# Reordering the prologue's loads: channel weights four tiles ahead, inputs before the first weight tile, five table buffers

## The chip, the core and the metric

The kernel runs on one core of a Trainium2 chip. It uses the core's five engines: TensorE (PE) for matrix products, VectorE (DVE) and ScalarE (ACT) for elementwise work and copies, GpSimd (POOL) for some elementwise work and for starting transfers, SyncE (SP) for starting transfers. Each engine works through its own list of instructions in the order in which the program gives them, and waits on semaphores for what the other engines and the transfers deliver. The metric is the device time of one execution in microseconds (us). Before the change it is 2592.13 us, the median of three runs (2591.88 to 2593.12).

## The reference

Two layers follow one another, on a batch of 8 sequences of 3008 positions by 256 features. The first multiplies each sequence's real Fourier spectrum by a filter. The second is a mixer block: a product along the positions, then one along the features.

```python
X = np.fft.rfft(x, axis=1)
y = np.fft.irfft(X * (filt_r + 1j * filt_i)[None], n=3008, axis=1)       # 8 x 3008 x 256

h  = np.maximum(y.transpose(0, 2, 1) @ w_tok1, 0.0) @ w_tok2             # 3008 -> 256 -> 3008
u  = y + h.transpose(0, 2, 1)
out = u + np.maximum(u @ w_ch1, 0.0) @ w_ch2                             # 256 -> 1536 -> 256
```

The weights arrive as 64-bit floats, seen by the kernel as pairs of 32-bit words, and have to be turned into 32-bit floats on the chip.

## The kernel before

The Fourier transforms are done as two small dense transforms (64 and 47 points) by TensorE. The kernel has two parts. A **prologue** transforms the first sequence (`dft(GROUPS[0])`), converts all weights and computes the first token products; then `mix` runs the mixer over all 8 sequences, with the transforms of the following sequences (`dft(GROUPS[1])` and so on) interleaved step by step.

**The weight tiles.** The weights are cut into 40 tiles, each handled by a Python generator with three stages: *begin* takes a staging buffer and starts the load, *copy* lets ScalarE read the high words, *end* lets VectorE finish the conversion (and, for channel weights, start what follows). Every call of `convert()` ends one tile, copies the next, and begins another.

```python
early = [(up, "u")] * 2 + [(tp, "t")] * 2 + [(vp, "v")] * 2
late = [(t2p, "t2"), (t3p, "t3")]                       # each pool has 2 buffers: 4 in all
stages = [(t4p, "t4")] * (A // 2) + early * 3 + late * 5     # 12 + 18 + 10 tiles

tiles = ([w1_load(i) for i in range(A // 2)] + [w2_load(i) for i in range(TC * N2 // NG)]   # 12 + 16
         + [wc1_load(c * (DC // 512), False) for c in range(DH)] + [f(i) for f, i in LAST]) # 2 + 10
begin, copy, end = iter(tiles), iter(tiles), iter(tiles)

def convert():
    ended[0] += 1
    while behind and behind[0][0] < ended[0] - 2:       # products of earlier tiles on TensorE
        behind.pop(0)[1]()
    advance(end)
    advance(copy)
    advance(begin)
```

Counting all calls of `advance(begin)`, six more than the number of converted tiles have been begun at any time: `convert()` number n ends tile n-1 and begins tile n+5 (tiles counted from 0). Tiles 30 to 39 (`LAST`) are staged in the four `t2` and `t3` buffers in turn, so tile 34 takes the buffer of tile 30.

**The channel weights.** Tiles 28 to 39 hold `w_ch1` and `w_ch2`. The mixer uses a fast matrix scheme with seven products, which needs sums of weight blocks. GpSimd makes them (`combine`, five operations for each of the 6 block columns `jp`, once for `chan[0]` and once for `chan[1]`). GpSimd also starts these tiles' loads.

```python
def combine(w):                                          # lines 331 to 339
    a11, a12, s4, na22, s3, s2, s1 = (w[:, :, n, :] for n in range(7))
    add = nc.gpsimd.tensor_tensor
    nc.gpsimd.tensor_scalar(out=na22, in0=s1, scalar1=-1.0, scalar2=None, op0=ALU.mult)   # L335
    add(out=s1, in0=s3, in1=s1, op=ALU.add)              # L336
    add(out=s3, in0=a11, in1=s3, op=ALU.subtract)        # L337
    add(out=s2, in0=s1, in1=a11, op=ALU.subtract)        # L338
    add(out=s4, in0=a12, in1=s2, op=ALU.subtract)        # L339

def wc1_load(i, late=True):
    c, q = divmod(i, DC // 512)
    st = stage(512)
    for g in range(CB):                                  # four loads, on GpSimd's queue (L345)
        nc.gpsimd.dma_start(st[ts(g, CW)], moe_w_ch1[ds((g * DH + c) * CW, CW), ts(q, 512)])
    yield
    yield from rounded(st, 512, [...], late)             # DVE L247 to L252, sum in L273
    if c == DH - 1:
        for jp in range(2 * q, 2 * q + 2):
            combine(chan[0][:, jp:jp + 1])

def wc2_load(i):                                         # one load (L356), one combine of chan[1]
    ...
```

**The first transform.** Twelve input tiles are loaded, half of each tile by SP and half by GpSimd; TensorE multiplies each (L419), ScalarE copies the result into `turned` (L422), and after six and after twelve tiles VectorE transposes half of `turned` (L459, eight instructions). Then 32 steps follow: `b_unit(k)` (L475 on TensorE, the products with the filter L487 to L489 on VectorE) and `bi_unit(k)` (L499 on TensorE, copy L505 on ScalarE). Each pair of steps needs a filter tile (`filt_load`, on GpSimd's queue, 3 buffers) and a table tile (`wb`, on SP's queue, 3 buffers).

```python
        def w_load(c):
            ...
                wbs[g] = wbp.tile([P, WC, P + KR], FP32, tag="wb", name="wb")
                nc.sync.dma_start(wbs[g], (wbi0_d if first else wbi_d)[:, ts(g, WC), :])
            filt_load(c, first)
        ...
        for k in range(K2 + 1):
            if k < K2:
                b_unit(k)
                if k % KC == 0 and k // KC + 2 < K2 // KC:
                    t2_load(k // KC + 2)
                    w_load(k // KC + 2)
                if first and k % KC == KC - 1 and k + 1 < K2:
                    filt_double(k // KC + 1)             # ACT L225
            if k >= 1:
                bi_unit(k - 1)
            yield
```

**The prologue's order.**

```python
        advance(begin)                                    # tile 0, ahead of the inputs
        for i, _ in enumerate(dft(GROUPS[0])):            # tile 1 is begun after six input tiles
            ...
            if i < NXC:                                   # NXC = 12 input tiles
                if i in (0, 2, 4, 6):
                    advance(begin)
                if i == 0:
                    advance(copy)
                if i in (NXC // 2 - 1, NXC - 1):
                    convert(); rounds += 1
            else:
                if (i - NXC) % 3 == 2:                    # eleven times in the 32 steps
                    convert(); rounds += 1
                k = i - NXC - 2
                if 19 <= k < 25:
                    t4_load(0, k - 19, 0, PARTS[1])       # into the buffers that staged tiles 5 to 10
                ...
        sum_up()
        for i in range(rounds, A // 2 + TC * N2 // NG):   # the rest, up to 28 converted tiles
            convert()
            ...
            if i == A // 2 + BY_PE - 1:
                sum_up()
                acc = token_sums(0)
        h1s[0] = token_relu(acc)
        for dh in range(DH):
            convert()                                     # tiles 28 and 29
            u_part(0, 0, dh)
```

In `mix`, each of the 6 x 6 items of a sequence is one `up_first` (L602), `up_middle`, `up_last` (L618), and the `down` products of the item before (L636); `convert()` is called twice in each item, ahead of `up_first` and ahead of `up_last`, until tile 39 is done (five items). VectorE's elementwise instructions of the mixer all stand in line 580.

Of the kernel before, what the change touches and what calls it, by code (L numbers as in the profile page):

```python
# [10 lines left out]
FP32 = mybir.dt.float32  # L11
# [12 lines left out]
P = 128  # L24
K2 = 32
A = 24
KR = 4 * A
HALF = 64
XC = 2
NXC = A // XC  # L30
# [3 lines left out]
KC = 2  # L34
WC = 2
# [89 lines left out]
def kernel(  # L125
# [32 lines left out]
    t1p = pool("t1p", 2)  # L158
    wbp = pool("wbp", 3)
# [48 lines left out]
    def filt_load(c, first):  # L208
        t, k0 = filts[c % FB], c * KC

        q = nc.gpsimd if first else nc.sync
        for src, i, p0 in ((filt_r, 0, 0), (filt_i, 1, HALF)) + (() if first else ((filt_r, 0, HALF),)):
            q.dma_start(t[p0:p0 + A, i], raw(src, k0, [[64 * D, A], [D, KC], [1, D]]))
            lo = p0 + 32
            if k0 == 0:
                q.dma_start(t[lo:lo + A, i, 0, :], raw(src, 32, [[64 * D, A], [1, D]]))
            k = max(k0, 1)

            for j0, n in ((0, 16), (16, A - 1 - 16)):
                q.dma_start(t[lo + j0:lo + j0 + n, i, k - k0:KC, :],  # L220
                            raw(src, 64 * (j0 + 1) - k, [[64 * D, n], [-D, k0 + KC - k], [1, D]]))
# [54 lines left out]
    ended = [0]  # L276
# [98 lines left out]
    def advance(it):  # L375
        s = next(it, None)
        if s:
            next(s, None)
# [5 lines left out]
    def convert():  # L384

        ended[0] += 1
        while behind and behind[0][0] < ended[0] - 2:
            behind.pop(0)[1]()
        advance(end)
        advance(copy)  # L390
        advance(begin)

# [22 lines left out]
    def a_unit(b, c):  # L417
        ps = bank(free_bank())
        nc.tensor.matmul(ps, wa0 if b == 0 else wa, xs.pop((b, c)).rearrange("p a d -> p (a d)"), start=True, stop=True)  # L419
        if b == 0:  # L420
            d0, c = divmod(c, NXC // 2)
            nc.scalar.copy(out=turned[:, ts(c, 2 * XC), ds(d0 * P, P)], in_=ps.rearrange("p (a d) -> p a d", d=P))  # L422
            return
        t1 = t1p.tile([P, XC, D], FP32, tag="t1", name="t1")
        nc.scalar.copy(out=t1.rearrange("p a d -> p (a d)"), in_=ps)
        nc.scalar.dma_start(rows_of(z_d, b)[:, ts(c, XC), :], t1)

    def dft(bs):
        first = bs[0] == 0
        nb = len(bs)  # L430
        todo = [(b, c) for b in bs for c in range(NXC)]
        wbs = {}

        def w_load(c):
            if c * KC % WC == 0:
                g = c * KC // WC
                wbs[g] = wbp.tile([P, WC, P + KR], FP32, tag="wb", name="wb")
                nc.sync.dma_start(wbs[g], (wbi0_d if first else wbi_d)[:, ts(g, WC), :])
            filt_load(c, first)

        ahead = NXC if first else XB
        for u in todo[0:ahead]:
            x_load(*u)
            if first and u[1] == NXC // 2 - 1:
                advance(begin)
        if not first:
            yield True
        for i, u in enumerate(todo):
            if first and i in (1, 4):
                w_load(i // 4)  # L450
            a_unit(*u)
            if i + ahead < len(todo):
                x_load(*todo[i + ahead])
            yield i + 1 < len(todo)
            if first and (i + 1) % (NXC // 2) == 0:

                for d in range(i // (NXC // 2) * P, (i + 1) // (NXC // 2) * P, 16):
                    v = turned.rearrange("p s d -> p d s")[:, d:d + 16, :]
                    nc.vector.transpose(v, v)  # L459
        t2s, t3s, prods = {}, {}, {}  # L460

        def t2_load(c):
            if first:
                return
            t2s[c] = t2p.tile([KR, KC, nb, D], FP32, tag="t2", name="t2")
            for i, b in enumerate(bs):
                nc.sync.dma_start(t2s[c][:, :, i, :], z_d[b, ts(c, KC)].rearrange("k r d -> r k d"))

        def b_unit(k):
            tag = ("b", "pg")[k % 2] if first else free_bank()  # L470
            if not first:
                held.append(tag)
            ps = bank(tag).rearrange("p (b d) -> p b d", b=2)[:, 0:nb, :]
            t2 = turned[:, k, :].unsqueeze(1) if first else t2s[k // KC][:, k % KC]
            nc.tensor.matmul(ps, wbs[k // WC][0:P if first else KR, k % WC, 0:P], t2, start=True, stop=True)  # L475
            re, im = slice(0, HALF), slice(HALF, P)
            t = filts[k // KC % FB]
            fr = t[:, 0, k % KC, :].unsqueeze(1).to_broadcast([P, nb, D])
            fi = t[im, 1, k % KC, :].unsqueeze(1).to_broadcast([HALF, nb, D])
            p1 = p1p.tile([P, 2 if first else nb, D], FP32, tag="p1", name="p1")  # L480
            if first:
                p1, p2 = p1[:, 0:1], p1[:, 1:2]
                prods[k] = (p1, p2)
            else:
                p2 = p2p.tile([P, nb, D], FP32, tag="p2", name="p2")
                prods[k] = (p1,)
            nc.vector.tensor_tensor(out=p1, in0=ps, in1=fr, op=ALU.mult)  # L487
            nc.vector.scalar_tensor_tensor(out=p2[re], in0=ps[im], scalar=-1.0, in1=fi, op0=ALU.mult, op1=ALU.mult)
            nc.vector.tensor_tensor(out=p2[im], in0=ps[re], in1=fi, op=ALU.mult)  # L489
            if not first:  # L490
                nc.vector.tensor_tensor(out=p1, in0=p1, in1=p2, op=ALU.add)  # L491

        def bi_unit(k):


            ps = bank("acc" if first else held.pop(0)).rearrange("p (b d) -> p b d", b=2)[:, 0:nb, :]
            parts = prods.pop(k)
            for i, p in enumerate(parts):
                nc.tensor.matmul(ps[0:KR], wbs[k // WC][:, k % WC, P:], p, start=(i == 0), stop=(i == len(parts) - 1))  # L499
            c, r = divmod(k, KC)  # L500
            if r == 0:
                where, tag = (p2p, "p2") if first and c % 3 == 2 else (t3p, "t3")
                t3s[c] = where.tile([KR, KC, nb, D], FP32, tag=tag, name="t3")

            nc.scalar.copy(out=t3s[c][:, r].rearrange("p b (e g i) -> p b g e i", e=DH, i=CW),  # L505
                           in_=ps[0:KR].rearrange("p b (g e i) -> p b g e i", e=DH, i=CW))
            if r == KC - 1:
                t3 = t3s.pop(c)
                for i, b in enumerate(bs):
                    nc.scalar.dma_start(g_d[b, ts(c, KC)].rearrange("k r d -> r k d"), t3[:, :, i, :])  # L510

        for c in range(2):
            t2_load(c)
            if not first:
                w_load(c)
        yield
        yield
        if first:
            filt_double(0)
        for k in range(K2 + 1):  # L520
            if k < K2:
                b_unit(k)
                if k % KC == 0 and k // KC + 2 < K2 // KC:
                    t2_load(k // KC + 2)
                    w_load(k // KC + 2)
                if first and k % KC == KC - 1 and k + 1 < K2:
                    filt_double(k // KC + 1)
            if k >= 1:
                bi_unit(k - 1)
            yield  # L530
# [241 lines left out]
    with tc.manual_schedule():  # L772
# [3 lines left out]
            nc.vector.memset(t, 0.0)  # L776
        rounds = 0
        second = dft(GROUPS[1])
        advance(begin)
        for i, _ in enumerate(dft(GROUPS[0])):  # L780
            if i == 0:
                for t, src in ((wai_t, wait_d), (wa, wa_d), (wai, wai_d), (ident, ident_d)):
                    nc.scalar.dma_start(t, src)

            if i < NXC:
                if i in (0, 2, 4, 6):
                    advance(begin)
                if i == 0:
                    advance(copy)
                if i in (NXC // 2 - 1, NXC - 1):  # L790
                    convert()
                    rounds += 1
            else:
                if (i - NXC) % 3 == 2:
                    convert()
                    rounds += 1

                k = i - NXC - 2
                if 19 <= k < 25:
                    t4_load(0, k - 19, 0, PARTS[1])  # L800
                elif k == 25:
                    next(second)
                elif k in (30, 31):
                    for c in range(3):
                        t4_load(0, 3 * (k - 30) + c, PARTS[1], PARTS[2])
# [68 lines left out]
```

## Time and profile before

| what | value |
| --- | --- |
| time, median of three | 2592.13 us |
| span of the profiled execution | 2589.4 us |
| TensorE busy, share of the span | 2508.9 us, 97% |
| VectorE busy | 1814.0 us, 70% |
| ScalarE busy | 691.1 us, 27% |
| GpSimd busy | 533.0 us, 21% |
| TensorE in us 0 to 40 | 17.78 us |
| TensorE in us 40 to 114 | 67.92 us of 74 |
| TensorE in us 161 to 229 | 50.88 us of 68, at a mean granted clock of 0.82 |
| TensorE in us 229 to 300 | 69.07 us of 71 |

The page of the profile gives the engines' busy times, the waits and the chain of work that ended last; the trace behind it gives every instruction with its start, its duration, the idle time before it and what ended that idle time. The span falls into a first stage (inputs, us 0 to 37), the 32 steps of the first transform (to about 114), the rest of the weights with the token products (to about 160), and the mixer.

### The profile page before, as it was taken

The page shows a single profiled execution, that of the slowest core. Times are in us where ns is not written, and L with a number is a line of the kernel's source. Part 1 is how long each engine was busy: PE and PEld are TensorE (multiplying, and loading weights), DVE is VectorE, ACT ScalarE, POOL GpSimd, SP SyncE. Part 2 cuts the span into 40 slices and gives each one's busy share as a digit, 9 for nine tenths or more (in the row PEclk, how much of TensorE's full clock was granted, in tenths as well). Part 3 has the DMA queues.
Part 4 walks back from the last instruction along what each step waited for, and adds up shares of the span by engine and source line. Part 5 has one row for each costly group of instructions (what it writes and reads, how often), then busy time and mean ns, then how long its engine had stood idle before and what let it go on. Part 6 is the DMA issues. An engine that isn't in the chain of part 4 may idle for free.

```text
span 2589.4 us, 31456 instructions
## 1 busy us (share of the span) xinstructions
PE 2508.9 (97%) x10952; PEld 2004.6 (77%) x10952; DVE 1814.0 (70%) x3458; ACT 691.1 (27%) x1347; POOL 533.0 (21%) x980
## 2 busy tenths in 40 slices
PE   6979999999999999999999999999999999999998
PEld 3556766788878777888787777788888888888887
DVE  7886888556675888746666788846678577647676
ACT  3423222123222222222221222212222122212222
POOL 5552111111211112112112111121121121211212
PEclk8989999999999999999999999999999999999999
DMA  9854333312332322203232223211232121100000
GB/s 214 234 155 140 110 101 110 106 48 86 94 90 63 88 84 75 80 15 91 90 95 78 75 84 86 81 31 57 90 85 74 50 64 53 25 9 8 17 12 21
DMA packets 153739, 205.21 MB, mean 79 GB/s; under 512 B 34232, under 2 KB 104994, under 8 KB 153580
## 3 DMA queue, kind: packets, MB, share of 16 engines
q1 hardware_dynamic: 82332, 114.08, 15.4%
q0 software_dynamic: 31296, 41.51, 6.6%
q10 hardware_dynamic: 39952, 47.61, 5.7%
q8 instruction: 87, 1.43, 0.2%
q14 instruction: 72, 0.59, 0.1%
HBM read 131.23 MB, written 71.83 MB: 78 GB/s over the span
## 4 chain that ended last, share of the span: by engine, by line
PE 79%; DVE 12%; DMA 3%; issue 2%; ACT 2%; POOL 1%; ACTq 0%; SPq 0%; DVEq 0%; POOLq 0%
PE ps_po L636 27%; PE ps_pg L602 16%; PE ps_pg L618 12%; PE ps_b L562 4%; PE ps_b L545 3%; DVE t L580 2%; PE ps_acc L545 2%; PE ps_acc L562 2%; DVE hh L580 2%; PE ps_acc L499 2%; PE ps_b L567 2%; PE ps_acc L419 2%; DVE u L580 1%; PE ps_b L499 1%; PE ps_b L475 1%
## 5 line engine op out<-in xcount | busy, mean ns | idle before, releaser
L580 DVE TENSOR_TENSOR hh<-ps_pg,s 128x512 f32<-128x512 f32 (+3 forms) x864 | 482.4, 586 | 633.9 <-ACT s L605 629.8
L681 POOL DMA_DIRECT2D out_dram<-r x757 | 411.2, 552 | 1947.1 <-ACT hh L623 928.6
L623 ACT ACTIVATE hh<-hh 128x512 f32<-128x512 f32 (+1 forms) x576 | 347.8, 621 | 1127.3 <-DVE hh L580 1127.3
L636 PE MATMUL ps_po<-t,wc 128*128 128x256 f32 (+1 forms) x2304 | 535.5, 375 | 5.0 <-DVE t L580 4.2
L636 PEld LDWEIGHTS ps_po<-t,wc 128*128 128x128 f32 x2304 | 434.5, 190 | 132.5 <-issue 53.5
L602 PE MATMUL ps_pg<-v,wc 128*128 128x256 f32 (+1 forms) x1728 | 416.2, 377 | 9.1 <-POOL wc L338 9.0
L636 PE MATMUL ps_po<-hh,wc 128*128 128x256 f32 (+1 forms) x1728 | 414.6, 376 | 6.0 <-POOL wc L339 5.7
L602 PEld LDWEIGHTS ps_pg<-v,wc 128*128 128x128 f32 x1728 | 328.4, 191 | 50.3 <-POOL wc L338 9.8
L636 PEld LDWEIGHTS ps_po<-hh,wc 128*128 128x128 f32 x1728 | 328.2, 190 | 45.9 <-POOL wc L339 6.8
L618 PE MATMUL ps_pg<-u,wc 128*128 128x256 f32 (+1 forms) x1152 | 295.1, 379 | 2.7 <-DVE hh L580 2.3
L580 DVE TENSOR_TENSOR t<-t,hh 128x256 f32<-128x256 f32 (+1 forms) x576 | 242.0, 420 | 19.8
L618 PEld LDWEIGHTS ps_pg<-u,wc 128*128 128x128 f32 x1152 | 217.0, 191 | 38.7 <-DVE hh L580 12.0
L580 DVE TENSOR_TENSOR s<-ps_pg,hh 128x512 f32<-128x512 f32 (+1 forms) x288 | 196.0, 681 | 32.3 <-PE ps_pg L602 1.8
L580 DVE TENSOR_TENSOR t<-hh 128x512 f32<-128x512 f32 (+1 forms) x288 | 192.0, 667 | 0.6 <-ACT hh L623 0.6
L602 PE MATMUL ps_pg<-u,wc 128*128 128x256 f32 (+1 forms) x576 | 169.9, 377 | 0.9 <-DVE hh L580 0.9
L618 PE MATMUL ps_pg<-v,wc 128*128 128x256 f32 (+1 forms) x576 | 169.7, 376 | 0.0
L605 ACT COPY s<-ps_pg 128x256 f32<-128x256 f32 (+1 forms) x288 | 106.0, 368 | 160.2 <-PE ps_pg L602 157.0
L618 PEld LDWEIGHTS ps_pg<-v,wc 128*128 128x128 f32 x576 | 109.2, 191 | 13.5
L602 PEld LDWEIGHTS ps_pg<-u,wc 128*128 128x128 f32 x576 | 102.6, 191 | 19.2 <-issue 8.9
L562 PE MATMUL ps_b<-w,h 128*128 128x512 f32 (+1 forms) x232 | 108.8, 592 | 0.0
L545 PE MATMUL ps_b<-t,w 128*128 128x256 f32 x480 | 104.5, 379 | 0.7 <-DMA t<-g_tmp 0.7
L499 PE MATMUL ps_acc<-p,wb 128*96 128x256 f32 (+1 forms) x256 | 95.0, 471 | 8.0 <-DVE p L491 3.7
(104 smaller groups left out, 2252.6 us busy)
## 6 DMA issues: line engine op xcount, KB each, us to landing
g_tmp<-t ACTq DMA_DIRECT2D x128, 192.0 KB
out_dram<-r POOLq DMA_DIRECT2D x698, 32.0 KB, 1.8
x<-in_x_dram SPq DMA_DIRECT2D x173, 128.0 KB
z_tmp<-t ACTq DMA_DIRECT2D x84, 256.0 KB
t<-z_tmp SPq DMA_DIRECT2D x112, 192.0 KB
t<-g_tmp SPq DMA_DIRECT2D x42, 512.0 KB
wb<-wbi_t SPq DMA_DIRECT2D x80, 224.0 KB
filt<-in_filt_r_dram SPq DMA_DIRECT2D x128, 48.0 KB
```

What stands on the lines that cost most here:

```text
L419: nc.tensor.matmul(ps, wa0 if b == 0 else wa, xs.pop((b, c)).rearrange("p a d -> p (a d)"), start=True, stop=True)
L499: nc.tensor.matmul(ps[0:KR], wbs[k // WC][:, k % WC, P:], p, start=(i == 0), stop=(i == len(parts) - 1))
L545: nc.tensor.matmul(acc[:, t, :], w1[:, a, ts(t, P)], t4[b, a // TC4][:, a % TC4, :], start=(a == 0 and t == 0), stop=(a == A - 1 and t == ...
L562: nc.tensor.matmul(ps[:, 0:w], h1[:, t, ts(dh, P)], w2[:, t, ds(m * 512, w)], start=(t == 0), stop=False)
L567: nc.tensor.matmul(ps[:, ds(q * P, n)], t4[b, c][:, r, ts(dh, P)], wai[:, 0:n], start=False, stop=(q == 3))
L580: nc.vector.tensor_tensor(out=out, in0=in0, in1=in1, op=op)
L602: nc.tensor.matmul(ps[:, 0:hw], chan[0][:, jp, n, :], mov, start=True, stop=True)
L605: nc.scalar.copy(out=s[:, 0], in_=g[0][:, 0, 0:hw])
L618: nc.tensor.matmul(ps[:, 0:hw], chan[0][:, jp, n, :], mov, start=True, stop=True)
L623: nc.scalar.activation(out=hs, in_=hs, func=AF.Relu)
L636: nc.tensor.matmul(po[i][:, j, 0:hw], chan[1][:, jp, n, :], mov, start=(jp == 0 and first == 1), stop=(jp == JP - 1 and last == 1))
L681: q.dma_start(rows[g, e, :, ds(h * A + 4 * m, n)], blocks[ts(g, CW), h, e, 0:n])
```

## The change

It touches the order of the prologue only; no instruction of the mixer and no arithmetic is changed.

1. **How far ahead tiles are begun.** A counter `begun` and a function `fill` replace the fixed order. Tiles 0 to 29 stay six ahead; tiles 30 to 39 are begun four ahead. It is meant to let GpSimd's combinations stand in its list before loads that wait for a buffer.
2. **Inputs first.** No weight tile is begun before the inputs; tile 0 takes the place between the sixth and the seventh input tile, tiles 1 to 4 are begun after input tiles 1, 3, 5 and 7, and three more with the first `convert()` of the 32 steps. The first stage converts one tile where it converted two; the second of those moves to the stage after the transform.
3. **Tables.** `table_load` is split from `filt_load`. Two of every five table tiles of the first transform go into the `t1` buffers, which nothing else uses then, so that five tables can be held and are loaded four pairs of steps ahead where it was two. The filter tiles stay two pairs ahead.

```diff
@@ convert
         advance(end)
         advance(copy)
+        fill(6)
+
+    begun = [0]
+
+    def fill(ahead):
+        while begun[0] < len(tiles) and begun[0] < ended[0] + (4 if begun[0] >= len(tiles) - len(LAST) else ahead):
+            start()
+
+    def start():
         advance(begin)
+        begun[0] += 1
@@ dft
-        def w_load(c):
+        def table_load(c):
             if c * KC % WC == 0:
                 g = c * KC // WC
-                wbs[g] = wbp.tile([P, WC, P + KR], FP32, tag="wb", name="wb")
+                where, tag = (t1p, "t1") if first and g % 5 > 2 else (wbp, "wb")
+                wbs[g] = where.tile([P, WC, P + KR], FP32, tag=tag, name="wb")
                 nc.sync.dma_start(wbs[g], (wbi0_d if first else wbi_d)[:, ts(g, WC), :])
+
+        def w_load(c):
+            table_load(c)
             filt_load(c, first)
@@
             if first and u[1] == NXC // 2 - 1:
-                advance(begin)
+                start()
@@
             if first and i in (1, 4):
                 w_load(i // 4)
+            if first and i in (7, 9):
+                table_load((i - 3) // 2)
@@
                     t2_load(k // KC + 2)
-                    w_load(k // KC + 2)
+                    if not first:
+                        w_load(k // KC + 2)
+                if first and k % KC == 0:
+                    if k // KC + 2 < K2 // KC:
+                        filt_load(k // KC + 2, first)
+                    if k // KC + 4 < K2 // KC:
+                        table_load(k // KC + 4)
@@ the prologue
-        advance(begin)
         for i, _ in enumerate(dft(GROUPS[0])):
@@
-                if i in (0, 2, 4, 6):
-                    advance(begin)
-                if i == 0:
+                if i in (1, 3, 5, 7):
+                    start()
+                if i in (NXC // 2 - 1, NXC - 1):
                     advance(copy)
-                if i in (NXC // 2 - 1, NXC - 1):
-                    convert()
+                if i == NXC // 2:
+                    ended[0] += 1
+                    advance(end)
                     rounds += 1
```

## The prediction

> **What bounds the kernel now.** I read the page's slices first. TensorE fills nearly every slice from the fourth on; only the start is thin.
>
> ```profile
> PE   6979999999999999999999999999999999999998
> PEclk8989999999999999999999999999999999999999
> ```
>
> A slice is 64.7 us, so slices 1 and 3 (us 0 to 65 and 130 to 194) have the gaps. After us 230 TensorE is busy 69.07 of 71 us (table by stage); the change touches nothing there, so what the prologue saves should move the whole mixer forward and reach the end one for one.
>
> Next the timeline of TensorE by instruction, in the stretch where channel weights are converted beside the first mixer items. The bracket is the idle time before the instruction and its releaser.
>
> ```profile
> 160.24 0.59 PE L602 MATMUL ps_pg<-u,wc 128*128 128x256 f32 x2
> 167.83 2.93 PE L602 MATMUL ps_pg<-v,wc 128*128 128x256 f32 x6 [7.00 <-POOL wc L338]
> 188.33 2.93 PE L602 MATMUL ps_pg<-v,wc 128*128 128x256 f32 x6 [2.00 <-POOL wc L338]
> 196.68 2.08 PE L636 MATMUL ps_po<-hh,wc 128*128 128x256 f32 x4 [4.57 <-POOL wc L339]
> 228.42 0.59 PE L602 MATMUL ps_pg<-u,wc 128*128 128x256 f32 x2
> ```
>
> TensorE waits three times for GpSimd's combinations, and the first six matmuls after a long wait take 2.93 us where the same six take 1.46 elsewhere. Items 0 to 4 last from 160.24 to 228.42. Why was GpSimd late? Its own timeline:
>
> ```profile
> 163.66 1.95 POOL L345 DMA_DIRECT2D st<-in_moe_w_ch_dram  x4 [11.69 <-DVE rest L252]
> 165.75 0.54 POOL L335 TENSOR_SCALAR wc<-wc 128x128 f32<-128x128 f32 x1
> 184.75 0.75 POOL L356 DMA_DIRECT2D st<-in_moe_w_ch_dram  x1 [3.87 <-issue]
> 185.53 0.55 POOL L335 TENSOR_SCALAR wc<-wc 128x128 f32<-128x128 f32 x1
> ```
>
> The combinations of block columns 0 and 1 stand behind the load of tile 34, and that load waits 11.69 us for VectorE to finish tile 30 (the same buffer). Their own input was there long before: VectorE wrote the last of tile 29 at 156.33 + 0.69 = 157.02. The other wait has the same form: the load at 184.75 (tile 37) waited for tile 33, whose last read ended at 184.18. VectorE in turn idles, waiting for matmuls that wait for GpSimd:
>
> ```profile
> 156.33 0.69 DVE L273 TENSOR_TENSOR wc<-both 128x512 f32<-128x512 f32 x1
> 162.42 0.69 DVE L252 SCALAR_TENSOR_TENSOR rest<-st,rest 128x512 f32<-128x512 uint32 x1
> 169.49 0.42 DVE L580 TENSOR_TENSOR hh<-ps_pg,s 128x256 f32<-128x256 f32 x1 [5.58 <-ACT s L605]
> 200.50 0.69 DVE L580 TENSOR_TENSOR hh<-ps_pg,s 128x512 f32<-128x512 f32 x1 [3.26 <-PE ps_pg L618]
> ```
>
> Two smaller places. In the first stage VectorE sets the end: its transposes finish at 28.79 + 8.54 = 37.33, and the first step's matmul starts at 37.43. At the end of the 32 steps a filter tile and a table tile come late:
>
> ```profile
> 17.98 8.70 DVE L459 STREAM_TRANSPOSE turned<-turned 128x512 f32<-128x512 f32 x8 [1.73 <-ACT turned L422]
> 28.79 8.54 DVE L459 STREAM_TRANSPOSE turned<-turned 128x512 f32<-128x512 f32 x8
> 96.87 0.43 DVE L488 SCALAR_TENSOR_TENSOR p<-ps_b,filt 64x256 f32<-64x256 f32 x1 [1.08 <-DMA filt<-in_filt_i_dram]
> 105.22 0.82 PE L475 MATMUL ps_b<-turned,wb 128*128 128x256 f32 x2 [1.78 <-DMA wb<-wbi_t]
> 105.14 0.62 ACT L225 COPY filt<-filt 64x512 f32<-64x512 f32 x1 [3.28 <-DMA filt<-in_filt_r_dram]
> ```
>
> **What the Trainium skill says.** "TensorE: Matmul & The Clock Gate", section "Architectural detail", says that ACT and DVE queues are strictly first-in first-out, and GpSimd's per core. The trace agrees: 2 us of ready combinations sat 8.7 us (157.02 to 165.75) behind a load. The same page, "What's actually happening", has the array's clock halved after an idle window: the 2.93 against 1.46 us. "SBUF — State Buffer", "SBUF: two separate sides", says that a VectorE operation with two SBUF inputs and a GpSimd operation exclude each other; the conversion's L248 takes 0.69 us alone (161.24) and 0.83 beside a combination (176.02). "DMA: Bandwidth & Descriptors", "Issuing engines are not separate DMA queues", says that all queues end on the same 16 transfer engines; in us 0 to 40 their share is about 1.0 at 205 to 219 GB/s.
>
> **The change, part by part.** The counts are by the program: no instruction is added or taken away, all is order.
>
> *Four ahead.* Tile 34's load now comes in `convert()` 31, after tile 30's end; the combinations of tile 29 come in `convert()` 30. They can start at about 157.1, and the fourth of them is done 2.2 us later (four starts from 165.75 to 167.32 plus 0.46 is 2.0), at about 159.3, before the mixer's sums `v` are ready (159.98 + 0.88 = 160.86). So the first wait goes wholly. The gain is not TensorE's 7.0 plus 2.0 plus 4.57: with the waits gone VectorE, which carries two conversions of about 3.1 us and some 4 us of mixer work per item, sets the pace. So I count VectorE's idle time that came from the waits: item 0, 5.58 plus 0.88; item 2, 0.31 plus 0.88 plus 3.26 plus 0.16; sum **11.1 us**. TensorE isn't in the way: it is busy 50.88 us of the stretch, slow-clock matmuls included, and after the gain 57 us remain.
>
> *Inputs first.* A first-layer weight tile is 64 x 2 x 4 KB = 0.52 MB, about 2.5 us at 205 GB/s. One of two goes out of the inputs' way. The first input landed at 9.08; the twelfth's copy ended at 27.89. Both should come 2 to 2.5 us earlier. The first transposes start then at about 15.3; after them VectorE ends tile 0 (before, tile 1 stood there: 26.57 to 28.87), then transposes again: 15.3 + 8.7 + 2.3 + 8.55 = 34.9 against 37.4, **gain 2.5**.
>
> *The moved conversion.* Before, tile 0 was ended in VectorE's idle time (13.90 to 16.24). Now one more tile is ended after the 32 steps, where VectorE is the limit: tiles 14 to 17 follow each other at 1.83 us (119.34, 121.17, 123.00). **Cost 1.8.**
>
> *Five tables.* The last table's load was issued at 97.79 and cost TensorE 1.78 us. It will now be there. But the filter tile of the same steps landed at 105.1 (the ScalarE line above), within 0.1 us of the table, and keeps its place. Without contention from the late table, one token weight tile fewer, and inputs of the next sequence pushed back behind a waiting token load, it may land a little sooner. The steps run at 6.46 us per three (48.96, 55.25, 62.15, 68.44 on VectorE); the last two groups lost about 0.9 and 3.5 us. I choose **2.0** of these 4.4.
>
> Sum: 11.1 + 2.5 - 1.8 + 2.0 = 13.8 us, so 2592.1 - 13.8 is about **2578.5 us**.
>
> **Rivals.** *The loads come too late.* Four ahead instead of six gives a channel load about three `convert()` calls before its copy. In the mixer a call comes every 5 us or so, and loads land in 2.5 to 7.5 us (median 4.5), so the data should be there; tile 33, now behind ten combinations of about 0.52 us, starts near 162.3, lands near 167 and is copied near 171. Were each of six late tiles 1 us late, the gain falls to about 8 us: 2584. *TensorE is the bound in items 3 and 4.* From 196.68 to 228.42 it idles under 2 us; if that isn't catching up but its true load, only about 9 of the 11.1 come: 2580.5. Against it: at most 51 us of work (50.88 busy, slow clock included) in 57. *The whole idle of TensorE comes back.* Then 13.6 us of waits for GpSimd and about 4 of slow clock go: 2572. *Tables are worth nothing,* the filter being as late as before, and the wait only changes its name: 2580.5. *A new stall on SP:* two token loads now wait for the stages of tiles 9 and 10, which end one group of steps later, and the next inputs stand behind them. They are needed only after the steps, so I expect no loss; if they delay the token products by 3 us, 2581.5.
>
> **Range and chances.** The mixer part is uncertain by about 3 us each way, the steps by 2, the first stage by 1, the arrival of the gain at the end by 3; together about 5, stretched towards a smaller gain: **2571 to 2587 us**. A change of 2% is 52 us, more than all of TensorE's idle time in us 0 to 300 (22.2 in the first 40, 28.9 in the 260 after); a loss of 2% would need a wait that nothing shows. Faster by over 2%: 0.01; within: 0.98; slower: 0.01.
>
> **What would show it.** GpSimd's line L335 of the first combination right after tile 29's last sum (near 153 if the stages before gain 2 to 3 us), ahead of any load that waits; no wait of over 1 us of L602 or L636 for L338 or L339; items 0 to 4 in about 57 us where they took 68.2. The first L475 near 35. No wait for `wb` in the steps, and at their end a wait for `filt` still, of 1 to 3 us. One more 1.83 us conversion before the token products. I am wrong if ScalarE or VectorE waits for channel loads, if a later stage gives the time back, or if items 0 to 4 stay slow with GpSimd on time.

## The result and the profile after

The changed kernel takes 2578.72 us, the median of four runs (2577.76 to 2581.47), against 2592.18 us for the kernel before in the same session. The ratio is 0.9949 with a 95% interval of 0.9932 to 0.9966: 13.5 us less. A second set of four runs, with a second profile (experiment 5), gave 2578.61 us and 0.9949 (0.9932 to 0.9965).

Its lines stand a little lower in the file than before: the combinations stay at L335 to L339, the mixer's matmuls are L624 (`up_first`), L640 (`up_last`) and L658 (`down`), VectorE's mixer work is L602, the transposes are L475, the steps' first matmul is L491.

GpSimd's timeline after, at the place where it had stood 11.69 us behind a load:

```profile
155.37 0.53 POOL L335 TENSOR_SCALAR wc<-wc 128x128 f32<-128x128 f32 x1 [5.79 <-DVE wc L273]
161.89 0.80 POOL L356 DMA_DIRECT2D st<-in_moe_w_ch_dram  x1
162.72 0.56 POOL L335 TENSOR_SCALAR wc<-wc 128x128 f32<-128x128 f32 x1
166.18 2.23 POOL L345 DMA_DIRECT2D st<-in_moe_w_ch_dram  x4
```

The releaser of the first combination is now its own input, VectorE's last sum of tile 29 (154.41 + 0.69 = 155.10, just below), and the loads come after the combinations. Nothing in this stretch of GpSimd's list waits for a buffer. TensorE and VectorE, in the same stretch:

```profile
157.06 0.59 PE L624 MATMUL ps_pg<-u,wc 128*128 128x256 f32 x2
157.95 1.56 PE L624 MATMUL ps_pg<-v,wc 128*128 128x256 f32 x6 [0.30 <-POOL wc L338]
162.53 1.99 PE L640 MATMUL ps_pg<-u,wc 128*128 128x256 f32 x4 [3.02 <-DVE hh L602]
183.29 1.13 PE L658 MATMUL ps_po<-hh,wc 128*128 128x256 f32 x4 [0.48 <-POOL wc L339]
216.87 0.59 PE L624 MATMUL ps_pg<-u,wc 128*128 128x256 f32 x2
154.41 0.69 DVE L273 TENSOR_TENSOR wc<-both 128x512 f32<-128x512 f32 x1
165.09 0.82 DVE L252 SCALAR_TENSOR_TENSOR rest<-st,rest 128x512 f32<-128x512 uint32 x1
```

The waits of 7.00, 2.00 and 4.57 us for L338 and L339 have become 0.30, 0.48 and, in item 3, 0.28; the first six matmuls of item 0 take 1.56 us where they took 2.93 (in items 2 and 4 of this profile they still take 2.50 and 2.39). In the second profile one longer wait for L339 is left, in item 2:

```profile
181.20 1.13 PE L658 MATMUL ps_po<-hh,wc 128*128 128x256 f32 x4 [1.95 <-POOL wc L339]
```

What TensorE now waits for in item 0 is VectorE (3.02 us in both profiles), which ends a tile between its mixer operations. Items 0 to 4 last from 157.06 to 216.87, 59.81 us for 68.18.

The first stage, on VectorE, in the first profile and then in the second:

```profile
14.94 8.61 DVE L475 STREAM_TRANSPOSE turned<-turned 128x512 f32<-128x512 f32 x8 [8.72 <-ACT turned L432]
29.44 8.60 DVE L475 STREAM_TRANSPOSE turned<-turned 128x512 f32<-128x512 f32 x8 [3.70 <-ACT turned L432]
```

```profile
13.55 8.62 DVE L475 STREAM_TRANSPOSE turned<-turned 128x512 f32<-128x512 f32 x8 [7.33 <-ACT turned L432]
26.62 8.60 DVE L475 STREAM_TRANSPOSE turned<-turned 128x512 f32<-128x512 f32 x8 [2.26 <-ACT turned L432]
```

The first half comes 3.0 and 4.4 us earlier than the 17.98 of before, but the second transposes now wait for inputs (3.70 and 2.26 us), which they hadn't done. The steps begin at 38.14 in one profile and at 35.32 in the other; before it was 37.43. In the steps the waits for `wb` and, in the last of them, for `filt` are gone.

The table cuts the span at the same events in each profile: the first matmul of the steps, the end of VectorE's last product with the filter, the first matmul of the `u` products (the second token product, just ahead of the mixer), the first matmul of items 0 and 5, the end.

| stretch | before | after, change in the two profiles |
| --- | --- | --- |
| to the first step | 37.43 | +0.7, -2.1 |
| the 32 steps | 74.79 | -4.8, -3.7 |
| to the `u` products (one more conversion) | 35.06 | +2.1, +1.8 |
| to item 0 | 12.96 | -1.3, -1.1 |
| items 0 to 4 | 68.18 | -8.4, -10.0 |
| item 5 to the end | 2360.98 | +1.9, +1.6 |
| span | 2589.4 | -9.7, -13.5 |

### The profile page after: what moved, and what is told of

It reads as the page before. It is cut to its first block, busy times and chain, and to the rows that moved or that the text cites. A ratio compares the mean times of both kernels' runs of the same rounds, so it can differ in the third digit from the quotient of the medians.

```text
span 2579.7 us, 31463 instructions
## 1 busy us (share of the span) xinstructions
PE 2506.2 (97%) x10952; PEld 2001.6 (78%) x10952; DVE 1816.7 (70%) x3458; ACT 690.8 (27%) x1347; POOL 534.0 (21%) x980
## 4 chain that ended last, share of the span: by engine, by line
PE 78%; DVE 14%; DMA 2%; issue 2%; ACT 2%; ACTq 1%; POOL 0%; SPq 0%; DVEq 0%; POOLq 0%
PE ps_po L658 27%; PE ps_pg L624 15%; PE ps_pg L640 12%; PE ps_b L584 4%; PE ps_b L567 3%; DVE t L602 3%; DVE hh L602 3%; PE ps_acc L515 3%; PE ps_acc L567 2%; PE ps_acc L584 2%; PE ps_b L589 2%; PE ps_acc L429 2%; DVE u L602 2%; PE ps_b L491 1%; DVE s L602 1%
## 5 line engine op out<-in xcount | busy, mean ns | idle before, releaser
L602 DVE TENSOR_TENSOR hh<-ps_pg,s 128x512 f32<-128x512 f32 (+3 forms) x864 | 482.6, 586 | 624.9 <-ACT s L627 624.1
L658 PE MATMUL ps_po<-t,wc 128*128 128x256 f32 (+1 forms) x2304 | 535.4, 375 | 5.3 <-DVE t L602 4.5
L658 PEld LDWEIGHTS ps_po<-t,wc 128*128 128x128 f32 x2304 | 434.6, 190 | 132.6 <-issue 53.3
L624 PE MATMUL ps_pg<-v,wc 128*128 128x256 f32 (+1 forms) x1728 | 415.4, 377 | 0.4 <-POOL wc L338 0.3
L658 PE MATMUL ps_po<-hh,wc 128*128 128x256 f32 (+1 forms) x1728 | 413.8, 375 | 1.1 <-POOL wc L339 0.8
L624 PEld LDWEIGHTS ps_pg<-v,wc 128*128 128x128 f32 x1728 | 328.2, 191 | 41.4 <-DVE v L602 3.0
L658 PEld LDWEIGHTS ps_po<-hh,wc 128*128 128x128 f32 x1728 | 327.6, 190 | 41.3 <-ACT s L627 1.9
L640 PE MATMUL ps_pg<-u,wc 128*128 128x256 f32 (+1 forms) x1152 | 294.5, 378 | 8.2 <-DVE hh L602 7.6
L602 DVE TENSOR_TENSOR t<-t,hh 128x256 f32<-128x256 f32 (+1 forms) x576 | 242.0, 420 | 19.8
L640 PEld LDWEIGHTS ps_pg<-u,wc 128*128 128x128 f32 x1152 | 216.1, 190 | 44.9 <-DVE hh L602 18.8
L602 DVE TENSOR_TENSOR s<-ps_pg,hh 128x512 f32<-128x512 f32 (+1 forms) x288 | 196.1, 681 | 31.4 <-PE ps_pg L624 1.0
L602 DVE TENSOR_TENSOR t<-hh 128x512 f32<-128x512 f32 (+1 forms) x288 | 192.5, 668 | 0.6 <-ACT hh L645 0.6
L624 PE MATMUL ps_pg<-u,wc 128*128 128x256 f32 (+1 forms) x576 | 170.6, 378 | 2.2 <-DVE hh L602 2.2
L640 PE MATMUL ps_pg<-v,wc 128*128 128x256 f32 (+1 forms) x576 | 169.2, 375 | 0.0
L640 PEld LDWEIGHTS ps_pg<-v,wc 128*128 128x128 f32 x576 | 108.9, 190 | 13.3
L624 PEld LDWEIGHTS ps_pg<-u,wc 128*128 128x128 f32 x576 | 102.7, 191 | 21.3 <-issue 8.4
```

Source lines behind the costliest of these rows:

```text
L602: nc.vector.tensor_tensor(out=out, in0=in0, in1=in1, op=op)
L624: nc.tensor.matmul(ps[:, 0:hw], chan[0][:, jp, n, :], mov, start=True, stop=True)
L640: nc.tensor.matmul(ps[:, 0:hw], chan[0][:, jp, n, :], mov, start=True, stop=True)
L658: nc.tensor.matmul(po[i][:, j, 0:hw], chan[1][:, jp, n, :], mov, start=(jp == 0 and first == 1), stop=(jp == JP - 1 and last == 1))
```

## The experiments

Time of the kernel before in the sets: 2591.54 us (1 to 4), 2592.23 us (5 to 8), 2592.20 us (9 to 12).

**1. Four ahead alone.** Kernel before, with

```diff
-        advance(begin)
+        if begun[0] < len(tiles) - len(LAST) or begun[0] < ended[0] + 4:
+            start()
```

> The kernel before with the channel weight tiles (30 to 39) begun four ahead and nothing else. My theory: this part carries most of the gain. Items 0 to 4 of the mixer take about 59 us where they took 68.2, and the time falls by 8 to 11 us, to 2581 to 2584. Rival (the gain is mostly the tables' and the inputs'): under 5 us, above 2587.

Measured: 2581.95 us, ratio 0.9960 (0.9945 to 0.9975), 9.6 us less. Items 0 to 4 take 59.87 us (159.70 to 219.57), and all earlier stretches are within 0.6 us of before except the `u` products (1.3 us shorter). So this part goes with about 70% of the gain: 8.3 us in the items, by the mechanism foreseen, and 1.3 us in the `u` products, which isn't its doing, since experiment 2, with tiles six ahead, has the same there (11.7 us for 13.0).

**2. Inputs first alone.** The changed kernel's order of the first stage, six ahead throughout, three table buffers, tables two pairs ahead.

> The kernel before with the inputs ahead of the first weight tile (one conversion moved from the first stage to the one after the steps), six ahead throughout, three table buffers. By the trace of the changed kernel this part costs: its first step began 0.7 us later than before, and the moved conversion adds 1.8 to 2.1, so 2594 to 2595. As I predicted it (2.5 gained, 1.8 paid) it would be 2591.5. Rival: it also thins the traffic at the end of the steps and takes the waits for filter and table there away, then 2590 or less.

Measured: 2596.65 us, ratio 1.0021 (1.0014 to 1.0028), 5.1 us more, worse than either theory. The first stage did what I had predicted: the steps begin at 35.46, 2.0 us earlier. But the steps then take 78.8 us for 74.8. A token load, below, is one of the `t4_load` transfers into the buffers that staged tiles 5 to 10. SP's and TensorE's timelines of this kernel at their end:

```profile
99.01 0.45 SPq L552 DMA_DIRECT2D t<-g_tmp  x1
99.55 2.47 SPq L418 DMA_DIRECT2D x<-in_x_dram  x4
102.11 0.54 SPq L448 DMA_DIRECT2D wb<-wbi_t  x1
```

```profile
107.67 1.22 PE L488 MATMUL ps_b<-turned,wb 128*128 128x256 f32 x2 [5.62 <-DMA wb<-wbi_t]
```

The last table stands in SP's list behind a token load (99.01) that waits for the buffer of tile 10, which is ended one group of steps later than before. The table leaves at 102.11 where it left at 97.79, and TensorE waits 5.62 us. This is the stall on SP that the prediction named as a rival. In the changed kernel it does no harm, because all tables have been started before it.

**3. Five tables alone.** Kernel before, with the hunks of `table_load` only.

> The kernel before with five table buffers, tables loaded four pairs ahead, and nothing else. Theory: the waits at the end of the steps (about 4.4 us over the even pace) go with the late table, 2587.5 to 2588.5. The predicted half of it: 2590. Rival (the filter tile of the last steps stays as late as the table was, 105 us): no gain, 2592.

Measured: 2589.63 us, ratio 0.9991 (0.9983 to 1.0000), 1.9 us less; the steps take 72.4 us, 2.4 less. No wait for a table is left, but VectorE and ScalarE still wait for filter tiles, among them 0.73 and 1.39 us in ScalarE's copies L225 near the end:

```profile
104.37 0.62 ACT L225 COPY filt<-filt 64x512 f32<-64x512 f32 x1 [1.39 <-DMA filt<-in_filt_r_dram]
```

That is the half that I had predicted, for the reason that I had given.

**4. Four ahead and five tables.** The edits of 1 and 3.

> Four ahead and five tables, without the inputs first. If the parts add up and the inputs' part costs 1.5 to 3 us, this is faster than the whole change: 2576 to 2578 against 2578.7. If the inputs' part brings something (as I predicted, 0.7 us), 2579 to 2580 or more.

Measured: 2579.64 us, ratio 0.9950 (0.9933 to 0.9967), 11.9 us less: the sum of 1 and 3 (11.5). The whole change is about 1 us better than this, within the spread. So inputs first costs 5.1 us when alone and nothing beside the tables: the two parts aren't independent, and 1, 2 and 3 add to 6.4 us where the change brings 13.5.

**5. The change again.** No edit.

> The changed kernel once more, unaltered, for a second profile and time beside these runs. The first profile fell on its slowest run and began the steps at 38.14, where the inputs-first part alone began them at 35.46, with the same order up to there. If the first stage only varies from run to run, this one starts between 35 and 38; if the four and five table loads in the same queue hold the inputs back, it starts at 38 again. Time 2577.5 to 2580.

Measured: 2578.61 us, steps beginning at 35.32. Experiments 6, 7, 9 and 10 share this first stage and begin at 37.04, 35.18, 36.06 and 36.30. The first stage varies from profile to profile by up to 3 us, where kernels with the old order stay within 37.38 to 37.65. With the first profile, this one and experiment 2 that makes seven profiles, 36.2 in the mean, a gain of 1.2 us.

**6. Five ahead.** In `fill`, `(5 if ...` for `(4 if ...`.

> The changed kernel with the channel tiles five ahead in place of four. With five, tile 34's load still comes after the combinations of tile 29 in GpSimd's list, and each later load waits for a tile whose own combination follows it anyway. If the loss was that combinations stand behind loads waiting for later tiles, five is as good as four: 2577.5 to 2580.5, no wait of over 1 us for L338 or L339. Rival (each tile further ahead costs through traffic or port contention): about half of the part's gain is lost, 2583.

Measured: 2579.64 us, ratio 0.9952 (0.9937 to 0.9967), the intervals all but the same. Items 0 to 4 take 59.51 us. GpSimd's first combination again follows its own input:

```profile
153.97 0.53 POOL L335 TENSOR_SCALAR wc<-wc 128x128 f32<-128x128 f32 x1 [4.46 <-DVE wc L273]
```

One wait of over 1 us is left, 1.54 us for L339 in item 2, where the changed kernel has 0.48 and 1.95. The loss has a threshold and is no slope: six ahead puts a waiting load in front of a ready combination, five and four don't.

**7. Three ahead.** `(3 if ...`.

> The changed kernel with the channel tiles three ahead. GpSimd's order is as good as with four, but a load has one convert call less before its copy. If loads have time in hand (they land in 2.5 to 7.5 us, a call in the mixer comes every 5 us), 2578 to 2580; rival (the loads come too late): ScalarE waits for channel loads and the time is 2581 to 2585.

Measured: 2581.72 us, ratio 0.9961 (0.9946 to 0.9976), 3 us more than with four. Items 0 to 4 take 61.53 us. The waits of this kernel in us 150 to 230 (in us in total, times, the longest), and then the same row of the changed kernel:

```profile
ACT top L245 <- DMA st<-in_moe_w_ch_dram: 19.6, 5, 6.6
```

```profile
ACT top L245 <- DMA st<-in_moe_w_ch_dram: 1.8, 1, 1.8
```

The rival of the prediction, loads that come too late, is real at three and all but absent at four. ScalarE's 19.6 us of waits go with about 3 us of time; why so little of it reaches the end isn't shown.

**8. The next sequence's inputs later.** Kernel of 4, with

```diff
-                elif k == 25:
+                elif k == 28:
                     next(second)
```

> Four ahead and five tables, without the inputs first, and the next sequences' first inputs loaded three steps later (k = 28 for k = 25). In the changed kernel those loads left at 101.2 because a token load ahead of them in SP's list waited; in the kernel with four ahead and tables alone they left at 95.8 and the filter tiles of the last steps were waited for (1.15, 0.87, 0.78 us on VectorE). If that traffic is what made the filter late, the waits at the end of the steps go here too, the steps take 71 to 72 us where they took 73.3, and the time is 2577 to 2578.5. Rival (the gain in the steps came from the fewer token weight tiles in flight): steps stay at 73, time stays at 2579.6.

Measured: 2579.06 us, ratio 0.9949 (0.9934 to 0.9964), which decides nothing: the inputs left at 95.34, as early as in 4 (95.77). In SP's list they stand right behind the same token load in both kernels, and that load waited 4.3 us for its buffer in both, until about 95; so a later place in the program moved nothing. (The next expectation says that nothing in SP's list waited there. It did.) Its steps took 72.2 us, so the two profiles (73.3 and 72.2) show the spread.

**9. The next sequence's inputs early in the changed kernel.** `next(second)` is moved from k = 25 to k = 24, ahead of the last token load of that group.

> The changed kernel with the next sequence's first inputs put ahead of the last waiting token load in SP's list, so that they leave at about 93 to 95 us instead of 99 to 101. The edit before this failed to move them, because nothing in SP's list waited there. If their traffic is what makes the filter tiles of the last steps late, waits for filt of 1 to 3 us in all come back on VectorE near 97 to 105, the steps take 72 to 73 us (70.0 and 71.1 in the changed kernel's two profiles) and the time is 2579.5 to 2581.5. Rival (fewer token weight tiles in flight, or the tables alone): steps stay at 70 to 71.

Measured: 2582.58 us, ratio 0.9963 (0.9950 to 0.9976), 4 us more than the change and more than expected. SP and VectorE:

```profile
93.01 2.47 SPq L418 DMA_DIRECT2D x<-in_x_dram  x4
104.00 0.42 DVE L503 TENSOR_TENSOR p<-ps_b,filt 128x256 f32<-128x256 f32 x1 [2.65 <-ACT filt L225]
```

The inputs leave at 93.01 for 99.4 and 101.2 in the changed kernel's profiles, the wait for the last filter tile is back with 2.65 us, and the steps take 74.7 us for 70.0 and 71.1. The token load behind them leaves when it did before (98.84, for 98.87 in the second profile). So the half megabyte of inputs does make the filter late when it leaves just before it.

**10. Without the combinations.** The changed kernel with

```diff
     def combine(w):
-        (five operations)
+        nc.gpsimd.memset(w[:, :, 2:4, :], 0.0)
+        nc.gpsimd.memset(w[:, :, 5, :], 0.0)
```

It leaves out the sums of the weight blocks, five GpSimd operations each time, so its time is that of less work.

> The changed kernel with GpSimd's combinations left out: the five operations are replaced by two clears of the same blocks, so the sums of weight blocks are missing from the output. It asks where 2 of the predicted 11.1 us of items 0 to 4 went (59.8 and 58.2 us measured, 57 predicted). If VectorE's operations with two SBUF inputs are held up by the combinations beside them (L248 0.83 us for 0.69), VectorE is busy 49 to 50 us in the items for 52.2 and they take 55 to 57 us. Rival (order of the work on VectorE and TensorE, not contention): 58 to 60 us as before.

Measured, in one run: 2574.94 us, items 0 to 4 in 54.63 us, a little under what was expected. VectorE's groups in the items, in the changed kernel (second profile) and here; the columns are count, busy time in us, mean ns:

```profile
L252 DVE SCALAR_TENSOR_TENSOR rest<-st,rest 128x512 f32<-128x512 uint32 x10 | 7.9, 786 | 0.3
L250 DVE TENSOR_SCALAR rest<-top 128x512 uint32<-128x512 uint32 x10 | 5.2, 522 | 0.3
L602 DVE TENSOR_TENSOR t<-hh 128x512 f32<-128x512 f32 x4 | 3.2, 808 | 0.0
```

```profile
L252 DVE SCALAR_TENSOR_TENSOR rest<-st,rest 128x512 f32<-128x512 uint32 x10 | 6.9, 693 | 0.3
L250 DVE TENSOR_SCALAR rest<-top 128x512 uint32<-128x512 uint32 x10 | 4.3, 426 | 0.3
L597 DVE TENSOR_TENSOR t<-hh 128x512 f32<-128x512 f32 x4 | 2.7, 682 | 0.0
```

VectorE is busy 48.07 us in the items without the combinations, 52.14 with them in the changed kernel, 49.91 in the kernel before, for the same 90 instructions. The combinations slow what runs beside them, and with GpSimd no longer waiting more of them run beside VectorE. (The 3.6 us between 58.21 and 54.63 are not all of this kind: the wait of 1.95 us for L339 is gone here too.)

**11. The next sequence's inputs from ScalarE's list.** Kernel of 8, those loads on `nc.scalar`.

> Four ahead and five tables with the first stage as before, and the next sequence's first two inputs started from ScalarE's list at k = 28, which delays them really, to about 101 us. If their traffic made the filter late, the steps take 71 us for 73.3 and 72.2, and the time is 2577 to 2578.5, a little under the whole change (2578.6 and 2578.7): the late inputs are the benefit and the moved conversion (2.1 us) is the price. Rival: 2579.5 as with the two parts alone.

Measured: 2583.33 us, ratio 0.9962 (0.9949 to 0.9974), worse than 4 and outside both expectations, and the steps take 76.5 us. VectorE and ScalarE:

```profile
100.31 0.43 DVE L501 SCALAR_TENSOR_TENSOR p<-ps_b,filt 64x256 f32<-64x256 f32 x1 [1.24 <-DMA filt<-in_filt_i_dram]
105.69 2.56 ACTq L415 DMA_DIRECT2D x<-in_x_dram  x4
108.43 0.62 ACT L225 COPY filt<-filt 64x512 f32<-64x512 f32 x1 [3.12 <-DMA x<-in_x_dram]
```

The inputs left only at 105.69, and their starting held ScalarE's list for 2.56 us, just ahead of its last filter copy (108.43). A filter tile was waited for at 100.31, long before they left. So with the old first stage the inputs aren't the only cause of late filter tiles; which of the other transfers matters too (one more token weight tile is in flight there, and the last token load leaves some 5 us earlier) stays open.

**12. No weight tile among the inputs.** The changed kernel with tile 0 begun after the twelfth input in place of the sixth, one copy and no `end` in the first stage.

> The changed kernel with no weight tile begun before all twelve inputs and none ended in the first stage (one more conversion after the steps). The sixth-to-seventh gap is the question: the seventh input's product began at 18.4 to 20.6 in the changed kernel and at 19.2 to 20.1 before. If tile 0's 0.52 MB ahead of it matter, it begins 1.5 to 2.5 us earlier, at 16.5 to 18.5, and the steps start at 33.5 to 34.5. Rival (the inputs' own small packets set the pace): 18.4 or later. Its whole time is 1 to 3 us longer than the changed kernel's for the conversion moved.

Measured, in one run: 2576.68 us, below each of the eight runs of the changed kernel (2577.39 to 2581.47), where I had expected 1 to 3 us more. TensorE, VectorE and SP of this kernel, then SP of the changed kernel (second profile):

```profile
13.81 1.02 PE L429 MATMUL ps_b<-x,turned 128*128 128x512 f32 x2
14.63 17.17 DVE L475 STREAM_TRANSPOSE turned<-turned 128x512 f32<-128x512 f32 x16 [8.40 <-ACT turned L432]
1.14 13.86 SPq L418 DMA_DIRECT2D x<-in_x_dram  x12
```

```profile
1.15 4.09 SPq L418 DMA_DIRECT2D x<-in_x_dram  x6
5.28 1.29 SPq L301 DMA_DIRECT2D st<-in_moe_w_tok_dram  x2
9.59 9.15 SPq L418 DMA_DIRECT2D x<-in_x_dram  x6
18.78 0.60 SPq L449 DMA_DIRECT2D wb<-wbi_t  x1
```

The seventh input's product starts at 13.81 where it starts at 18.82 in the changed kernel, the sixteen transposes run without a gap, and the steps begin at 31.89. That is 3.4 us ahead of the second profile; the extra conversion takes back 2.4 us (39.28 us from the last product to the `u` products, for 36.89). Tile 0's 0.52 MB among the inputs cost the later ones 5.0 us, twice what its bytes take at 205 GB/s, and in SP's line of the changed kernel the loads after it are 1.5 us apart on average where the first six are 0.7 apart. What SP waited for in us 0 to 21 (in us in total, times, the longest), in the changed kernel (second profile) and then here:

```profile
SPq L418 <- DMA x<-in_x_dram: 3.6, 2, 3.0
SPq L418 <- DMA wai_t<-wait_t: 3.2, 1, 3.2
SPq L418 <- DMA st<-in_moe_w_tok_dram: 1.4, 1, 1.4
```

```profile
SPq L418 <- DMA x<-in_x_dram: 3.9, 2, 2.0
SPq L418 <- DMA wai_t<-wait_t: 2.1, 1, 2.1
```

These are no waits for a buffer. The trace gives each load's semaphore: the loads of SP and ScalarE share eight of them, and a load is started only when the one that had its semaphore before has landed. Tile 0's two loads take two of these eight places. So in the changed kernel the seventh input left at 9.59, when the fifth had landed (9.57), and here at 5.26: 4.3 us of the delay arise before the load starts. The ninth input waited in the same way for half of tile 0 (landed at 12.86, left at 12.88), the tenth for a table that ScalarE loads (`wai_t`, 16.71 and 16.73).

This kernel is the fastest complete kernel of the study, on one run without an interval.

## Why the prediction was right, and where only in its sum

The time was right to 0.2 us (2578.5 for 2578.7). That close it is luck: the parts, which add to 2578.3 when taken exactly, hide errors that cancel. By its own steps, with the second profile's value and the first's in brackets:

- **Four ahead: 11.1 predicted, 10.0 (8.4) measured; experiment 1 gives 8.3 in the items and 9.6 in time.** The mechanism is shown by 1 and 6: combinations behind a load that waits, with a threshold between five and six. The sum over VectorE's idle time was nearly the right size: within the items that idle time fell by 12.2 us (10.6). The term left out is that the freed combinations slow VectorE: its busy time in the items went from 49.91 to 52.14 us (52.16), and without them it is 48.07 (experiment 10). That takes back 2.2 us. The 1.6 us between the two profiles go with TensorE's granted clock in the items, 0.97 in the second and 0.91 in the first. The signs named came true, with one exception: in the second profile one `down` still waits 1.95 us for L339. Before the change TensorE waited four times and not three: the lines shown leave out 1.11 us for L339 at 178.68.
- **Inputs first: 2.5 predicted, 2.1 (-0.7) measured, 1.2 on the mean of seven profiles.** The first half did come early, by 4.4 us (3.0). The step that failed is that "both should come 2 to 2.5 us earlier": the twelfth input's copy ended at 26.59 (29.40), for 27.89. The working took a tile to cost its bytes. But a tile still stands between the sixth and the seventh input, tile 0 where tile 1 stood, and it holds two of the eight places for loads in flight (experiment 12): the seventh input left SP at 9.59 (10.93), for 10.60 before. In the first profile TensorE then sat idle 6.28 us, came back at its slow clock, and the seventh to twelfth products took over 8 us. This agrees with the Trainium skill ("TensorE: Matmul & The Clock Gate", "What's actually happening"), which halves the clock after an idle window: their starts are 1.7 to 1.8 us apart at first and 0.86 us apart at the end.
- **The moved conversion: 1.8 predicted, 1.8 (2.1) measured.** Right, and 2 shows the same 2.2 us.
- **Five tables: 2.0 predicted, 3.7 (4.8) measured in the steps.** Alone they bring 1.9 us of time and 2.4 in the steps, about as predicted (experiment 3). The size of what was to be had was read a little high: on VectorE the last two groups (94.03 to 101.41 to 110.91) lost 0.9 and 3.0 us, not 0.9 and 3.5. The rest is what inputs first and tables do together: the stalled token load holds the next inputs back until the filter tiles are under way. The prediction had both halves: the later inputs as a small help without a price, the stall as a rival at 3 us, but for another place (the token products). Experiment 9 undoes it and loses 4 us; in experiment 2 the same stall makes the steps 4 us longer, because a table stands behind it. Experiment 11 warns that the inputs aren't the only cause. The sign "at their end a wait for filt still, of 1 to 3 us" was wrong: there was none in either profile.
- **What wasn't in the sum.** The stretch between the `u` products' first matmul and item 0 became 1.1 to 1.3 us shorter. Its matmuls after TensorE's wait of 2.8 us for VectorE run partly at the slow clock, and how many of them varies: before, the first group took 2.07 us and the last four matmuls 2.92; in the first profile after it is 2.07 and 1.88, in the second 1.12 and 2.88. So most of this is where the clock happened to rise, and no part of the change: experiment 2, six ahead, has the short stretch too (11.7 us), and experiment 11, four ahead, the long one (13.1). And the mixer after item 5 took 1.6 to 1.9 us longer. The kernels with the inputs first, experiment 12 apart, lose about 0.4 us there in each of three places, whichever other parts they have; the cause stays open. Apart from that the gain reached the end one for one, as assumed.

In the second profile, then, 1.1 and 0.4 us too much in the first two terms stand against 1.7 too little in the tables, and the 1.1 gained before item 0 against the 1.6 lost after item 5. The range of 2571 to 2587 us was fair; the parts taken singly were known to about 2 us each, and two of them were not independent.

## What to carry to other kernels

An engine that both starts transfers and computes should compute first: put a load behind the work that is ready, or at least never further ahead than the buffers allow without waiting, because a waiting load holds everything behind it in the same list (here 8.7 us). Here the distance had a hard edge on one side (six tiles, with four buffers) and a softer one on the other (three tiles, loads late). When two parts of a change share a queue, try them together as well as singly: here a stall that made the steps 4 us longer in one company went with steps 2 to 4 us shorter in the other.

## What the runs showed that I had not expected

A weight tile of 0.52 MB between the sixth and the seventh input delays the seventh by 5.0 us (experiment 12, one run): no load there waits for a buffer, but each waits for one of eight semaphores to come free. GpSimd's operations slow not only VectorE's two-input ones beside them (L252, 693 to 786 ns in the mean) but also L250, which reads one tensor from SBUF (426 to 522 ns); the Trainium skill ("SBUF — State Buffer", "SBUF: two separate sides") names two-input operations and a faster mode of the others, and says that the loser blocks fully, while the single delays seen here are 0.1 to 0.3 us. And the first stage's length varies by 3 us between executions in the new order, by 0.3 us in the old one. A weight tile stands between the sixth and the seventh input in both, so that alone isn't the reason, which isn't shown.
